# Two layers of experts behind a Fourier filter: the second layer's sums of activations wait for the next pair

## The chip, the cores and the metric

The kernel runs on one core of one Trainium2 chip. The metric is the device time of one execution in microseconds (us); the time given for a version is the median of its runs. The profile is of one further execution.

## The reference

An input of 2 x 3008 x 256 goes through a spectral filter (a Fourier transform along the sequence, a complex matrix of 256 x 256 with soft threshold, the transform back). The 6016 rows then go through two layers of dense experts, in float32. The change touches the second one alone:

```
silu = g * (1.0 / (1.0 + np.exp(-g)))      # g   = x @ w_gate, 256 -> 1536
val = x @ w_val                            # val = x @ w_val,  256 -> 1536
return (silu * val @ w_out)                # 1536 -> 256
```

## The kernel before, in words

A matrix product in float32 is made of three products of rounded parts: each operand is split in a high part (a cast on ACT) and a low part (full minus high, on DVE, `low`), and PE multiplies low x high, high x high and high x low (`mm3`). So one "product" below is three matmuls of 128 x 128 weights on up to 512 columns.

The second layer works through 6 **pairs** of token blocks (two blocks of 512 columns; 448 in the last pair), and in each pair through 12 **quads**, one per 128 of the 1536 hidden features. A quad (`quad`, one call) multiplies the 2 x 2 arrangement of (gate, value) by (two halves of 256 inputs) by (two blocks) with 7 products instead of 8, on sums that were formed beforehand. Its weights come as a slot of 18 tiles of 128 x 128 (1152 KB): 14 for the seven products, 4 for the output layer. There are four slots, fetched two quads ahead from a scratch tensor in HBM (`Wd`) that the first layer's part of the program has written.

Two quads, an even and an odd one, make a **step**: their four gated activations (two features' groups by two blocks) are again a 2 x 2 arrangement, and the output layer takes 7 products for it too. Three of them are multiplied in the step itself, or one step later (`live`, into PSUM banks `acc1`, `acc2`, `acc4`). The other four need sums of activations and sums of output weights. The activations' operands lie in `units` tiles (13 of them, two steps each, taken and given back in turn) until the *next* pair, where `part2` splits one into parts per quad and `later` multiplies it, two halves per quad, with a `chunk` of weight sums from the scratch tensor `Vd`.

The sums of output weights are formed once, during the first pair. `ask_out(k)` reads the four output tiles of a step from `Wd`: a plain DMA (issued by SP) brings the high parts, and an accumulating DMA (issued by POOL) adds the low parts on top, after the first has landed. `out_sums` forms four sums on DVE, `out_parts` splits them and writes them to `Vd`. `ask_out(k + 1)` stands behind `out_parts(k)` in the odd quad.

The sums of activations: the even quad gives T1 (`times2` at its end) and T3 (`upper`, in the next quad); the odd quad gives V, a buffer of its own, and B22. T1 is cast and multiplied, then an accumulating DMA adds T3 to it. T2 = B22 + T1 is formed on DVE (`second_t`), an accumulating DMA adds T2 to V, and V is then cast and multiplied once more as "T4". V itself was multiplied before that. A third accumulating DMA adds B22 to T3 (`upper`).

Every engine takes its instructions in the order in which this code records them (the order is written by hand); an instruction waits on semaphores, and all behind it on its engine waits too. SP and POOL issue DMAs in their own order. `last` multiplies the four late products of the last pair when no quad is left.

Lines that matter below: L937 to L939 the matmuls of a quad's products, L132 to L134 those of `live`, L1166 to L1168 those of `later`; L1291, L1305, L1331 ACT copies of a product (to Q, c7, cu); L1343 and L1361 the DVE adds that end a gate; L1344 and L1366 the silu on ACT; L1261 the cast of a live operand; L1141 the cast in `part2`; L1150 the copy of the first output product at a pair's end (`begin`); L1212 the accumulating read of output weights; L1242, L1256, L1264 the accumulating DMAs into V, T3 and T1.

Of the kernel before, what the change touches and what calls it, by code (L numbers as in the profile page):

```python
# [82 lines left out]
def fourier_moe_kernel(ctx: ExitStack, tc: tile.TileContext, x, lin, bias, w1, w2, fwd1, inv2, fwd2,  # L83
# [612 lines left out]
    class Convert2(Convert):  # L696
# [10 lines left out]
        def steps(self):  # L707
# [6 lines left out]
            for i in range(n + 1):  # L714
# [21 lines left out]
                nc.scalar.copy(t[:, 14:16], O)  # L736
                low(t[:, 7:14], F[:, 1:], t[:, :7])
                yield
                low(t[:, 16:], O, t[:, 14:16])
# [346 lines left out]
    LATER = ("T2", "T1", "B22", "T3")  # L1086
# [4 lines left out]
    def lay_out():  # L1091
        ring2["c"] = Ring(xs_p.tile([128, 3, BLK], F32, tag="ct", name="cc", bufs=1), 0, 3)
        st = [wst.tile([128, BLK], t, tag="st", name="hv", bufs=5) for t in (F32,) * 4 + (F32R,)]
        spots.update(h=st[:2], V=st[2:4], lo=st[4:])

    def lay_out_rest():
        s = [cv.tile([128, BLK], t, tag="s", name="live", bufs=3) for t in (F32R, F32R, F32R)]
# [4 lines left out]
        spots.update(hi=s[1:], v=r[:1], w=r[1:2], short=r[2:], hi2=[c[:, 0:2], c[:, 2:4]], lo2=[c[:, 4:6], e[:, :2]])  # L1102
# [14 lines left out]
    def live(p, m, k, w, e, x):  # L1117
        if k == 0:
            acc[p, m] = acc_bank([128, BLK], f"acc{m}")
        mm3(acc[p, m][:, : halves[p]], w[:, 14 + e], w[:, 16 + e], *x, k == 0, k == KF2 // 2 - 1)  # L1120
# [25 lines left out]
    def begin(p):  # L1146
        n = halves[p]
        D = C[p, "D"] = one_bank(spot[0], [128, BLK], "D")
        a = acc.pop((p, 1))
        nc.scalar.copy(D[:, :n], a[:, :n])  # L1150
        c = C[p, "short"] = take("short")
        nc.scalar.copy(c[:, :n], a[:, :n])

    def later(p, i, half, D=None):
        m, kk = divmod(i, 3)
        n = halves[p]
        hi, lo = mid[p, i]
        w = mid[p, i, "w"]
        k = 2 * kk + half
        if m == 3 and k == 0:  # L1160
            C[p, "E"] = one_bank(spot[0] if D is None else D, [128, BLK], "E")
        o = C[p, "E" if m == 3 else "D"]
        wh, wl = w[:, 2 * half], w[:, 2 * half + 1]
        o, xh, xl = pairwise(o[:, :n]), woven(hi[:, half]), woven(lo[:, half])
        start = m == 3 and k == 0
# [9 lines left out]
    def phase(p, m):  # L1175
        n = halves[p]
        D = C[p, "E" if m == 3 else "D"][:, :n]
        if m == 0:
            v = C[p, "v"][:, :n]
            nc.vector.tensor_tensor(out=v, in0=D, in1=v, op=ALU.subtract)  # L1180
        elif m == 1:
            c = C[p, "w"] = take("w")
            nc.scalar.copy(c[:, :n], D)
        elif m == 2:
            c = take("short")
            nc.scalar.copy(c[:, :n], D)
            send_out(p, 0, 1, c)
        else:
            for name, e, t in (("w", 1, 1), ("v", 1, 0)):
                c = C.pop((p, name))  # L1190
                nc.vector.tensor_tensor(out=c[:, :n], in0=D, in1=c[:, :n], op=ALU.add)
                send_out(p, e, t, c)

    def corner(p):
        n = halves[p]
        c = C.pop((p, "short"))
        nc.vector.tensor_tensor(out=c[:, :n], in0=c[:, :n], in1=acc.pop((p, 2))[:, :n], op=ALU.subtract)
        send_out(p, 0, 0, c)

    def fourth(p):  # L1200
        n = halves[p]
        c = C[p, "v"] = take("v")
        nc.scalar.copy(c[:, :n], acc.pop((p, 4))[:, :n])

    G = {}

    def ask_out(k):
        F = G[k] = cv.tile([128, 8, 128], F32, tag="full", name="outs", bufs=2)
        for i in range(2):
            t = F[:, 2 * i : 2 * i + 2].rearrange("p a b -> p (a b)")  # L1210
            nc.sync.dma_start(t, Wd[2 * k + i][:, 14 * 128 : 16 * 128])
            nc.gpsimd.dma_start(t, Wd[2 * k + i][:, 16 * 128 :], accum_op=ALU.add)  # L1212

    def out_sums(k):
        F = G[k]

        def minus(o, x, y, sign=1):
            if sign > 0:
                nc.vector.tensor_tensor(out=F[:, o], in0=F[:, x], in1=F[:, y], op=ALU.subtract)
            else:  # L1220
                nc.vector.scalar_tensor_tensor(out=F[:, o], in0=F[:, x], scalar=-1.0, in1=F[:, y], op0=ALU.mult,
                                               op1=ALU.subtract)

        minus(5, 1, 3, -1)
        minus(4, 5, 0, -1)
        minus(6, 2, 4)
# [254 lines left out]
```

## Time and profile before

| | |
|---|---|
| median of the runs shown | 1233.7 us (1233.08 the lowest) |
| profiled execution | 1236.13 us, span 1234.3 us |
| mean granted TensorE clock | 0.968 |
| busy over the span | PE 92%, DVE 78%, ACT 67%, POOL 12% |
| DMA | 264.29 MB; SP's queue 53.1%, POOL's 14.8% of 16 engines' span |
| second layer's quads | from 614.76 us to 1197.86 us, then the tail |

The span is the time from the first to the last instruction; the execution's own time lies 1.8 us above it. PE's busy time says little of its pace: matmuls are pipelined, so the distance of their starts is what counts. A share of 1.00 of the DMA engines would be all 16 at work all the time.

### The profile page before, as it was taken

What the parts mean: (1) busy time and instruction counts of PE and PEld (TensorE: products, weight loads), DVE (VectorE), ACT (ScalarE), POOL (GpSimd) and SP (SyncE); (2) the same over time, 40 slices, a digit from 0 to 9 for tenths busy, and PEclk for the clock granted to TensorE, in tenths of its full rate; (3) what the DMA queues carried; (4) which work ended last, traced back from release to release, by engine and by line L of the source; (5) the groups of instructions that cost most, each with busy time, mean ns of one, the idle gap of its engine ahead of it and who ended that gap; (6) DMA issues with size and microseconds to landing.
All of it is one profiled execution on the core that took longest, in us unless ns stands there. A gap on an engine that the chain in (4) does not pass through costs nothing.

```text
span 1234.3 us, 20183 instructions
## 1 busy us (share of the span) xinstructions
PE 1136.3 (92%) x7362; PEld 979.7 (79%) x7362; DVE 962.1 (78%) x1677; ACT 823.8 (67%) x1500; POOL 148.6 (12%) x189
## 2 busy tenths in 40 slices
PE   9999999999999999999967568999999999998896
PEld 8988888888888888889955457877777777778874
DVE  6878888999999999999845356887777776776674
ACT  4767666787878877877744246675666666665663
POOL 3000026000000000000012111111111111111120
PEclk9999999999999999999988879999999999998997
DMA  8756339654735637355467869888888888888873
GB/s 306 273 172 202 111 96 302 221 184 127 263 134 172 228 126 248 137 179 206 133 200 201 207 166 294 251 275 274 249 261 274 237 259 273 239 261 242 265 200 114
DMA packets 95307, 264.29 MB, mean 214 GB/s; under 512 B 9316, under 2 KB 35204, under 8 KB 83752
## 3 DMA queue, kind: packets, MB, share of 16 engines
q1 hardware_dynamic: 76048, 227.32, 53.1%
q0 software_dynamic: 19008, 35.59, 14.8%
q8 instruction: 58, 0.95, 0.3%
q14 instruction: 41, 0.34, 0.1%
q10 hardware_dynamic: 152, 0.08, 0.0%
HBM read 191.99 MB, written 43.25 MB: 191 GB/s over the span
## 4 chain that ended last, share of the span: by engine, by line
PE 65%; DMA 16%; DVE 8%; ACT 6%; issue 4%; POOL 0%; SPq 0%; ACTq 0%; DVEq 0%; POOLq 0%
DMA hv<-units 9%; PE acc L132 7%; PE acc L134 7%; PE acc L133 7%; PE P L937 6%; PE P L939 5%; PE P L938 5%; DMA outs<-Wd 5%; PE Tb L937 3%; PE Tb L939 3%; PE Tb L938 3%; PE p L367 1%; PE p L461 1%; PE Q L937 1%; PE p L577 1%
## 5 line engine op out<-in xcount | busy, mean ns | idle before, releaser
L1344 ACT ACTIVATE hv<-hv 128x512 f32<-128x512 f32 (+1 forms) x72 | 44.8, 622 | 146.2 <-DVE hv L1343 146.2
L617 ACT CAST gated<-r 128x512 fp32r<-128x512 f32 (+1 forms) x160 | 98.1, 613 | 64.8 <-DVE r L985 63.3
L137 DVE TENSOR_TENSOR gated<-r,gated 128x512 fp32r<-128x512 f32 (+1 forms) x160 | 107.8, 674 | 23.9 <-ACT gated L617 19.1
L132 PE MATMUL acc<-gated,w_o 128*128 128x512 f32 (+1 forms) x320 | 120.4, 376 | 0.0
L133 PE MATMUL acc<-gated,w_o 128*128 128x512 f32 (+1 forms) x320 | 119.6, 374 | 0.0
L134 PE MATMUL acc<-gated,w_o 128*128 128x512 f32 (+1 forms) x320 | 119.6, 374 | 0.0
L937 PE MATMUL P<-xo,slot 128*128 128x512 f32 (+1 forms) x240 | 92.8, 387 | 2.7 <-DVE hold L989 1.2
L981 ACT ACTIVATE r<-hold,consts 128x512 f32<-128x512 f32 (+1 forms) x120 | 85.5, 713 | 13.9 <-DVE hold L989 11.8
L938 PE MATMUL P<-xo,slot 128*128 128x512 f32 (+1 forms) x240 | 90.2, 376 | 0.0
L939 PE MATMUL P<-xo,slot 128*128 128x512 f32 (+1 forms) x240 | 90.1, 375 | 0.0
L985 DVE SCALAR_TENSOR_TENSOR r<-r,hold 128x512 f32<-128x512 f32 (+1 forms) x120 | 80.8, 673 | 2.5 <-ACT r L981 1.4
L1261 ACT CAST live<-hv 128x512 fp32r<-128x512 f32 (+1 forms) x72 | 43.8, 609 | 54.2 <-DMA hv<-units 54.2
L1141 ACT CAST parts<-units 128x1024 fp32r<-128x1024 f32 (+1 forms) x72 | 74.2, 1032 | 7.7 <-PE E L1167 3.9
L937 PE MATMUL P<-gs,slot 128*128 128x512 f32 x104 | 43.2, 416 | 35.7 <-DVE hv L1361 34.7
L132 PEld LDWEIGHTS acc<-gated,w_o 128*128 128x128 f32 x320 | 60.5, 189 | 7.0
L134 PEld LDWEIGHTS acc<-gated,w_o 128*128 128x128 f32 x320 | 60.5, 189 | 6.9
L133 PEld LDWEIGHTS acc<-gated,w_o 128*128 128x128 f32 x320 | 60.5, 189 | 6.7
L137 DVE TENSOR_TENSOR parts<-units,parts 128x1024 fp32r<-128x1024 f32 (+1 forms) x36 | 43.2, 1201 | 24.2 <-ACT parts L1141 24.2
L1361 DVE TENSOR_TENSOR hv<-P,cc 128x512 f32<-128x512 f32 (+1 forms) x72 | 48.6, 675 | 17.2 <-PE P L939 16.8
L1212 POOL DMA_DIRECT2D outs<-Wd x12 | 10.8, 1038 | 420.5 <-ACT r L981 394.8
L137 DVE TENSOR_TENSOR hv<-hv,live 128x512 fp32r<-128x512 f32 (+1 forms) x35 | 23.8, 680 | 47.5 <-ACT live L1261 47.5
L1256 POOL DMA_DIRECT2D units<-units x36 | 33.5, 931 | 224.1 <-DVE units L1246 216.4
(241 smaller groups left out, 3528.3 us busy)
## 6 DMA issues: line engine op xcount, KB each, us to landing
slot<-Wd SPq DMA_DIRECT2D x72, 1152.0 KB
slot<-Sd SPq DMA_DIRECT2D x40, 896.0 KB
chunk<-Vd SPq DMA_DIRECT2D x72, 256.0 KB
st<-in_w SPq DMA_DIRECT2D x68, 256.0 KB
units<-units POOLq DMA_DIRECT2D x60, 256.0 KB, 3.9
Wd<-slot SPq DMA_DIRECT2D x12, 1152.0 KB
hv<-units POOLq DMA_DIRECT2D x30, 256.0 KB, 7.1
m<-in_fwd SPq DMA_DIRECT2D x12, 512.0 KB
```

What stands on the lines that cost most here:

```text
L132: nc.tensor.matmul(o, wl, xh, start=start, stop=False)
L133: nc.tensor.matmul(o, wh, xh, start=False, stop=False)
L134: nc.tensor.matmul(o, wh, xl, start=False, stop=stop)
L137: nc.vector.tensor_tensor(out=o, in0=full, in1=hi.bitcast(F32), op=ALU.subtract)
L617: nc.scalar.copy(hi[:, :n], g[:, :n])
L937: nc.tensor.matmul(o, wl, hi, start=start, stop=False, skip_group_check=not start)
L938: nc.tensor.matmul(o, wh, lo, start=False, stop=False, skip_group_check=not start)
L939: nc.tensor.matmul(o, wh, hi, start=False, stop=True, skip_group_check=not start)
L981: nc.scalar.activation(r[:, :n], x[:, :n], AF.Relu, bias=three)
L985: nc.vector.scalar_tensor_tensor(out=r[:, :n], in0=r[:, :n], scalar=6.0, in1=x[:, :n], op0=ALU.min, op1=ALU.mult)
L1141: nc.scalar.copy(hi, t[:, :, :n])
L1361: nc.vector.tensor_tensor(out=h1[:, :n], in0=P[:, :n], in1=c7, op=ALU.add)
```

## The change

In the first layer's part, the four output tiles of an odd or even group are stored per output half (high, low, high, low) instead of (high, high, low, low). A fetch takes 16 of 18 tiles for even quads and in all quads of the first pair; the last two tiles of an odd group's slot are overwritten, in the first pair, with a sum of output weights that `out_sums` forms as a fifth result (`fourth`).

The three products of a step that are multiplied at once are now T1, T4 and T2, each as it comes from its own product (in the step itself, and in the next step's even quad). The four for the next pair are T1 + T3, T2 + (T1 + T3), T3 + T2 and T4 + that T2, all formed in place in `units`: two by accumulating DMAs (`add_apart`), two by DVE (`add_up`). V and its buffers are gone; the buffers serve `ask_out`, which reads two steps at the start and then stands in the even quad behind `out_sums`, for two steps (four quads) later. In the output, `phase`, `corner` and `third` combine the seven products in another order; all four late products now go into one PSUM bank, except at the very end, where `E` takes one. In even quads `later`'s second half moves ahead of product 7, and both live products stand in the even quad.

```
@@ fetch @@
-            nc.sync.dma_start(slot[q][:, :c].bitcast(F32).rearrange("p a b -> p (a b)"), src)
+            if stream[q][0] == 2 and (stream[q][1] % 2 == 0 or q < len(quads1) + KF2):
+                c = 16
+            nc.sync.dma_start(slot[q][:, :c].bitcast(F32).rearrange("p a b -> p (a b)"), src[:, : c * 128])
...
-    LATER = ("T2", "T1", "B22", "T3")
+    LATER = ("T1", "T2", "T3", "T4")
...
@@ ask_out, out_sums, out_parts @@
     def ask_out(k):
-        F = G[k] = cv.tile([128, 8, 128], F32, tag="full", name="outs", bufs=2)
+        F[k] = take("outs").rearrange("p (a b) -> p a b", b=128)
         for i in range(2):
-            t = F[:, 2 * i : 2 * i + 2].rearrange("p a b -> p (a b)")
-            nc.sync.dma_start(t, Wd[2 * k + i][:, 14 * 128 : 16 * 128])
-            nc.gpsimd.dma_start(t, Wd[2 * k + i][:, 16 * 128 :], accum_op=ALU.add)
+            t = F[k][:, 2 * i : 2 * i + 2]
+            w = Wd[2 * k + i][:, 14 * 128 :].rearrange("p (e h c) -> p e h c", e=2, h=2)
+            nc.sync.dma_start(t, w[:, :, 0])
+            nc.gpsimd.dma_start(t, w[:, :, 1], accum_op=ALU.add)
...
-        minus(5, 1, 3, -1)
-        minus(4, 5, 0, -1)
-        minus(6, 2, 4)
-        minus(7, 0, 1)
+        nc.scalar.mul(g[:, 3], A[:, 3], -1.0)
+        minus(g[:, 0], A[:, 1], A[:, 3], -1)
+        minus(g[:, 1], g[:, 0], A[:, 0], -1)
+        minus(g[:, 2], A[:, 0], A[:, 1])
+        minus(g[:, 4], A[:, 2], g[:, 1])
+        if k + 2 < KF2 // 2:
+            ask_out(k + 2)
...
+        low(f[:, 1], g[:, 4], f[:, 0])
         nc.sync.dma_start(Vd[:, :, k], t.bitcast(F32).rearrange("p m i c -> p m (i c)"))
+        nc.sync.dma_start(Wd[2 * k + 1][:, 16 * 128 :], f.bitcast(F32).rearrange("p i c -> p (i c)"))
...
-    def second_t(p, k):
-        u, v = U(p, "T2", k), state[p, "V"]
-        sub_tile(U(p, "B22", k), U(p, "T1", k), u, ALU.add)
-        nc.gpsimd.dma_start(v, u, accum_op=ALU.add)
+    def add_up(p, k, to, x):
+        o = U(p, to, k)
+        nc.vector.tensor_tensor(out=o, in0=o, in1=U(p, x, k), op=ALU.add)
+
+    def add_apart(p, k, to, x):
+        nc.gpsimd.dma_start(U(p, to, k), U(p, x, k), accum_op=ALU.add)
...
@@ upper, halve @@
-        o = U(p, ("T3", "B22")[odd], k)
-        times2(o, h[:, :n], P[:, :n], 1 if odd else -1)
-        if odd:
-            nc.gpsimd.dma_start(U(p, "T3", k), o, accum_op=ALU.add)
+        times2(U(p, ("T3", "T2")[odd], k), h[:, :n], P[:, :n], 1 if odd else -1)
...
-        if what == "T1":
-            nc.gpsimd.dma_start(x, U(p, "T3", k), accum_op=ALU.add)
@@ quad @@
+        if old >= 0:
+            later(old, i, 1)
         if odd:
-            if old >= 0:
-                later(old, i, 1)
-            x[1] = halve(p, k, "T1")
-            if pv >= 0:
-                x[4] = halve(pv, kv, "T4")
-        elif pv >= 0:
-            x[2] = halve(pv, kv, "V")
-        T = one_bank(spot[0] + 3, [128, BLK], "Tb")
-        product(T, 7, start=True)
+            x1 = halve(p, k, "T1")
+            add_apart(p, k, "T1", "T3")
+            if a[0] >= 0:
+                add_up(*a, "T2", "T1")
+                add_apart(*a, "T4", "T2")
+        elif a[0] >= 0:
+            x2, x3 = halve(*a, "T4"), halve(*a, "T2")
+            add_up(*a, "T3", "T2")
+        if old >= 0 and i % 3 == 2:
+            phase(old, i // 3)
+        if old >= 0:
+            product(T, 7, start=True)
...
-        if not odd and pv >= 0:
-            second_t(pv, kv)
...
         if odd:
-            live(p, 1, k, slot[F0 + q - 1], 0, x[1])
+            live(p, 1, k, slot[F0 + q - 1][:, 14:16], x1)
             free.append(slot.pop(F0 + q - 1))
-        elif pv >= 0:
-            live(pv, 2, kv, slot[F0 + q - 1], 0, x[2])
+            fetch(F0 + q + ASK)
+        elif a[0] >= 0:
+            live(a[0], 2, a[1], slot[F0 + q - 1][:, 14:16], x2)
...
-                live(pv, 4, kv, slot[F0 + q - 2], 1, x[4])
-                free.append(slot.pop(F0 + q - 2))
...
-        elif old >= 0:
-            later(old, i, 1)
+        if not odd and a[0] >= 0:
+            live(a[0], 3, a[1], slot[F0 + q - 1][:, 16:18] if a[0] else fourth[a[1]], x3)
+            free.append(slot.pop(F0 + q - 1))
...
@@ last @@
-        order = (0, 1, 2, 9, 3, 4, 5, 10, 6, 7, 8, 11)
+        order = (0, 1, 2, 3, 4, 5, 9, 6, 7, 8, 10, 11)
...
     lay_out()
     ask_out(0)
+    ask_out(1)
```

POOL's order at the start of the first pair. L1212 before and L1216 after are the accumulating reads of output weights (`Wd_63` and `Wd_64` are the first step's); the other rows are accumulating DMAs of activations. Before:

```order
L1212 DMA outs<-Wd_63 128x256
L1212 DMA outs<-Wd_64 128x256
L1264 DMA units<-units 128x512
L1212 DMA outs<-Wd_65 128x256
L1212 DMA outs<-Wd_66 128x256
L1256 DMA units<-units 128x512
L1242 DMA hv<-units 128x512
L1264 DMA units<-units 128x512
```

And now:

```order
L1216 DMA hv<-Wd_63 128x2x128
L1216 DMA hv<-Wd_64 128x2x128
L1216 DMA hv<-Wd_65 128x2x128
L1216 DMA hv<-Wd_66 128x2x128
L1216 DMA hv<-Wd_67 128x2x128
L1216 DMA hv<-Wd_68 128x2x128
L1254 DMA units<-units 128x512
L1216 DMA hv<-Wd_69 128x2x128
L1216 DMA hv<-Wd_70 128x2x128
L1254 DMA units<-units 128x512 x2
```

The reads of three steps now stand ahead of the first sum of activations, and of the three accumulating DMAs per step two are left.

ACT's order in a later pair, around an odd quad before (`CAST live<-units` is T1, the next `CAST live<-hv` is V after its transfer, `cc<-Tb` the copy that frees product 7's bank for product 4):

```order
L1291 COPY Q<-P 128x512
L1261 CAST live<-units 128x512
L1261 CAST live<-hv 128x512
L1305 COPY cc<-Tb 128x512
L1141 CAST parts_7181<-units 128x1024
L1331 COPY cc<-P 128x512
```

And now, around an even quad (the two casts are T4 and T2):

```order
L1299 COPY Q<-P 128x512
L1270 CAST live<-units 128x512 x2
L1318 COPY cc<-Tb 128x512
L1145 CAST parts_7190<-units 128x1024
L1338 COPY cc<-P 128x512
```

No cast of a live operand reads a tile that a DMA has added to; in odd quads one cast is left.

DVE's order from an odd quad's end through the next even quad, before (L1237 is T2 = B22 + T1):

```order
L1246 TENSOR_TENSOR units<-hv,P 128x512
L137 TENSOR_TENSOR live<-hv,live 128x512
L1237 TENSOR_TENSOR units<-units 128x512
L137 TENSOR_TENSOR lows<-units,parts_7181 128x1024
L1343 TENSOR_TENSOR hv<-Tb,cc 128x512
L1361 TENSOR_TENSOR hv<-P,cc 128x512
```

And now (L1251 is T3 = T3 + T2, in place):

```order
L1258 TENSOR_TENSOR units<-hv,P 128x512
L137 TENSOR_TENSOR live<-units,live 128x512
L137 TENSOR_TENSOR lows<-units,live 128x512
L1251 TENSOR_TENSOR units<-units 128x512
L137 TENSOR_TENSOR lows<-units,parts_7190 128x1024
L1351 TENSOR_TENSOR hv<-Tb,cc 128x512
L1364 TENSOR_TENSOR hv<-P,cc 128x512
```

One low part came over from the odd quad; the add in place writes T3, which the DMA T1 = T1 + T3 of the quad before reads. The odd quad has the other add in place.

## Rows read from the trace of the kernel before

**Rows 1.** Busy time of each engine in stretches, clock, DMA share.

```profile
core 0: us, PE busy (x) PEld busy (x) DVE busy (x) ACT busy (x) POOL busy (x), PEclk, DMA share, GB/s
614.76:741.81 127.05, 84.91 (x324) 67.09 (x323) 64.53 (x116) 53.12 (x95) 23.12 (x26) 0.83 0.71 192
741.81:831.30 89.49, 84.75 (x378) 69.99 (x378) 69.38 (x100) 60.35 (x103) 15.70 (x18) 1.00 0.88 270
...
923.50:1017.19 93.69, 86.81 (x378) 72.91 (x378) 69.40 (x101) 60.84 (x103) 15.69 (x18) 0.96 0.85 258
...
1110.17:1197.86 87.69, 79.61 (x377) 72.27 (x378) 58.85 (x90) 53.28 (x96) 15.72 (x18) 0.96 0.82 243
1197.86:1234.30 36.44, 22.40 (x80) 16.93 (x79) 16.48 (x20) 13.43 (x19) 1.74 (x2) 0.79 0.39 117
745.00:780.00 35.00, 32.23 (x145) 26.34 (x144) 26.16 (x38) 22.13 (x38) 6.98 (x8) 1.00 0.93 302
411.40:492.80 81.40, 81.40 (x541) 70.39 (x543) 77.07 (x144) 65.00 (x114) 0.00 (x0) 1.00 0.56 188
```

**Rows 2.** PE's waits, first pair: for whom, us, times, longest.

```profile
PE P L937 <- DVE hv L1361: 34.7, 6, 7.4
PE P L937 <- DMA slot<-Wd: 5.6, 4, 2.4
```

**Rows 3.** Chain of waits, one step of the first pair: start, us.

```profile
672.31 3.08 DMA outs<-Wd
676.49 9.62 DMA outs<-Wd
688.60 0.79 PE P L937
```

**Rows 4.** Landing of L1212, the accumulating read of output weights.

```profile
DMA to landing us min/median/max: 3.1/9.1/10.2
```

**Rows 5.** Landing of L1264, T1 = T1 + T3.

```profile
DMA to landing us min/median/max: 3.1/3.3/8.3
```

**Rows 6.** Landing of L1256, T3 = T3 + B22.

```profile
DMA to landing us min/median/max: 3.1/6.3/10.5
```

**Rows 7.** PE's timeline in a later pair: start, us, instruction [idle before].

```profile
937.75 0.48 PE L937 MATMUL Tb<-xo,slot 128*128 128x512 f32 x1 [2.34 <-ACT cc L1305]
...
939.77 0.63 PE L938 MATMUL P<-xo,slot 128*128 128x512 f32 x1
...
943.50 0.38 PE L937 MATMUL Tb<-xo,slot 128*128 128x512 f32 x1
...
957.10 0.38 PE L937 MATMUL Tb<-xo,slot 128*128 128x512 f32 x1
```

**Rows 8.** ACT's timeline at the same place.

```profile
936.60 0.62 ACT L1261 CAST live<-hv 128x512 fp32r<-128x512 f32 x1 [3.65 <-DMA hv<-units]
937.12 0.58 ACT L1305 COPY cc<-Tb 128x512 f32<-128x512 f32 x1
```

**Rows 9.** PE's waits from 923.50 to 1017.19, a later pair.

```profile
PE Tb L937 <- ACT cc L1305: 5.5, 3, 2.3
PE D L1166 <- ACT D L1150: 1.3, 1, 1.3
```

**Rows 10.** DMA queues in the first pair: packets, MB, share of 16 engines.

```profile
q1 hardware_dynamic: 7166, 18.78, 45.2%
q0 software_dynamic: 3744, 5.51, 25.3%
```

**Rows 11.** POOL's DMA queue from 741.81 to 1197.86, five later pairs.

```profile
q0 software_dynamic: 12960, 23.07, 28.5%
```

**Rows 12.** POOL's timeline in a later pair.

```profile
952.16 0.87 POOL L1264 DMA_DIRECT2D units<-units  x1 [5.08 <-DVE lows L137]
```

**Rows 13.** DVE's timeline in the same step.

```profile
958.66 0.68 DVE L1237 TENSOR_TENSOR units<-units 128x512 f32<-128x512 f32 x1
```

**Rows 14.** PE's timeline in the tail.

```profile
1206.07 0.74 PE L132 MATMUL acc<-live,slot 128*128 128x448 f32 x1 [3.72 <-ACT live L1261]
```

More of the change, by code (lines that the diff above doesn't have):

```diff
@@ L1176, in phase @@
         n = halves[p]
-        D = C[p, "E" if m == 3 else "D"][:, :n]
+        D, one, three = C[p, 0][:, :n], C[p, "one"][:, :n], C[p, "three"][:, :n]
         if m == 0:
-            v = C[p, "v"][:, :n]
-            nc.vector.tensor_tensor(out=v, in0=D, in1=v, op=ALU.subtract)
+            nc.vector.tensor_tensor(out=one, in0=D, in1=one, op=ALU.subtract)
         elif m == 1:
-            c = C[p, "w"] = take("w")
-            nc.scalar.copy(c[:, :n], D)
+            nc.vector.tensor_tensor(out=three, in0=D, in1=three, op=ALU.add)
+            send_out(p, 0, 1, three)
@@ L1184, in phase @@
         elif m == 2:
-            c = take("short")
-            nc.scalar.copy(c[:, :n], D)
-            send_out(p, 0, 1, c)
-        else:
[L1189 to L1192, printed above, removed]
+            c = take("short")[:, :n]
+            nc.scalar.copy(c, D)
+            send_out(p, 1, 1, c)
+            if (p, "end") in C:
+                nc.vector.tensor_tensor(out=one, in0=D, in1=one, op=ALU.subtract)
+        elif (p, "end") in C:
+            nc.vector.tensor_tensor(out=one, in0=C[p, 3][:, :n], in1=one, op=ALU.add)
+            send_out(p, 1, 0, one)
+        else:
+            c = take("short")[:, :n]
+            nc.vector.tensor_tensor(out=c, in0=D, in1=one, op=ALU.subtract)
+            send_out(p, 1, 0, c)
@@ L1194, in corner, with third @@
     def corner(p):
         n = halves[p]
-        c = C.pop((p, "short"))
-        nc.vector.tensor_tensor(out=c[:, :n], in0=c[:, :n], in1=acc.pop((p, 2))[:, :n], op=ALU.subtract)
+        c = take("short")[:, :n]
+        nc.vector.tensor_tensor(out=c, in0=C[p, "one"][:, :n], in1=acc.pop((p, 2))[:, :n], op=ALU.subtract)
         send_out(p, 0, 0, c)
-    def fourth(p):
+    def third(p):
         n = halves[p]
-        c = C[p, "v"] = take("v")
-        nc.scalar.copy(c[:, :n], acc.pop((p, 4))[:, :n])
@@ L1269, in mark @@
         nc.tensor.matmul(o, slot[F0][:, 0], B[len(pairs)][1][:, 0], start=True, stop=True)
+    NK = KF2 // 2
     def quad(q, before):
@@ L1375, in last @@
         w = slot[F0 + len(quads2) - 1]
-        order = (0, 1, 2, 9, 3, 4, 5, 10, 6, 7, 8, 11)
+        order = (0, 1, 2, 3, 4, 5, 9, 6, 7, 8, 10, 11)
+        C[p, "end"] = True
+        C[p, 3] = one_bank(spot[0] + 4, [128, BLK], "E")
         def both(at):
-            i = order[at]
             for half in range(2):
-                later(p, i, half, spot[0] + 4)
-            if i % 3 == 2:
-                phase(p, i // 3)
-        def prepare(at):
-            if at > 1:
-                ask(p, order[at])
-            part2(p, order[at])
-        upper(before)
-        x = halve(p, k, "V")
-        both(0)
-        ask(p, 2)
-        part2(p, 1)
-        second_t(p, k)
-        live(p, 2, k, w, 0, x)
-        both(1)
-        part2(p, 2)
-        corner(p)
-        ask(p, order[3])
-        x = halve(p, k, "T4")
-        live(p, 4, k, w, 1, x)
-        fourth(p)
-        for at in range(2, 12):
+                later(p, order[at], half)
             if at + 2 < 12:
                 ask(p, order[at + 2])
+        both(0)
+        upper(before)
+        part2(p, 1)
+        x2 = halve(p, k, "T4")
+        both(1)
+        x3 = halve(p, k, "T2")
+        add_up(p, k, "T3", "T2")
+        add_up(p, k, "T2", "T1")
+        add_apart(p, k, "T4", "T2")
+        part2(p, 2)
+        live(p, 2, k, w[:, 14:16], x2)
+        both(2)
+        live(p, 3, k, w[:, 16:18], x3)
+        corner(p)
+        third(p)
+        phase(p, 0)
+        part2(p, 3)
+        for at in range(3, 12):
             both(at)
```

106 lines of the change are left out of this document (48 added, 58 removed).

## The prediction, made before the changed kernel ran

> **What bounds the kernel now.** I first cut the span into stages, each ending where a pair's first output product is copied out (ACT L1150), and read busy time, clock and DMA share of each [rows 1]. In the last pair of the first part PE is busy 81.40 of 81.40 us, with DVE at 77.07: PE can run without a gap beside a nearly full DVE. The second part does not reach that. Its first pair takes 127.05 us with PE busy 84.91 and a mean granted clock of 0.83; the next five take 87.69 to 93.69 us, the tail 36.44.
>
> Next, who PE waits for. In the first pair, 34.7 us in 6 waits go to the DVE add L1361 and 5.6 us to weights that have not landed [rows 2]. L1361 is not slow: the chain of waits runs from the weight sums through two transfers, 3.08 and 9.62 us, one after the other, to PE [rows 3]; the accumulating one lands after a median of 9.1 us [rows 4]. They are asked for in the quad before the one in which DVE wants them, and DVE works in order, so all behind them stands still. In a later pair PE waits 5.5 us in 3 waits for the ACT copy L1305, and 1.3 us at the border of the pairs [rows 9]. L1305 stands behind the ACT cast of V, which waited 3.65 us for V's accumulating transfer [rows 8]. Such a gap is paid twice: after 2.34 us of it matmuls take 0.63 us, the 1.2 GHz level, and only later 0.38 us again, the 2.4 GHz level [rows 7].
>
> The floor: 63 matmuls (an even and an odd quad) run from 943.50 to 957.10 without a gap [rows 7], 0.216 us each. A later pair has 378 [rows 1]: 81.6 us, and 82.9 with the border wait, which the change leaves. The first pair has 306 and finishes 42 narrower ones of the first part (448 columns, scaled to 0.189 us): 74 us.
>
> **The change, part by part.** *Weight sums asked for four quads ahead, first pair.* The two stages of reading (plain, then accumulating) had one quad of time and get four; even at 6.5 us a quad that is 26 us against the 3.1 + 9.6 of [rows 3]. So the 34.7 us go, with the half clock behind them. Next late are the DMA engines. Their share of 0.71 over 127.05 us is 90.2 us of work [rows 1]. The accumulating queue had 32.1 us of it [rows 10]. In five later pairs it spent 28.5% of 456.05 us on 90 transfers of 256 KB [rows 11], 1.44 us each; 16 such stand in the first pair (of 5.51 MB in all), which leaves 0.91 us for each of its 10 of 128 KB. After the change there are 11 of the large ones and 8 of the small, now in runs of 512 B instead of 1 KB. That run length is not in the trace; I bound it by no change (0.91) and by double (1.82), and take 1.1 since half of the bytes (the landing side) keep their layout: 24.6 us, or 7.5 less. The plain queue moved 18.78 MB in 57.4 us [rows 10], 0.327 MB per us. Twelve fetches lose 0.131 MB each (-4.8 us), one step's plain reads fall before the pair (-0.8), six writes of the fourth sum come (+2.4), and shorter runs cost between 0 and 3.2, taken as 0.8: 2.4 less. DMA work is then 80.3 us, more than PE's 74. The Trainium skill ("DMA: Bandwidth & Descriptors", Specifications) says that 512 B is the least size that still runs at line rate; by it the two surcharges vanish and 80.3 becomes 78. The best long stretch of before had a share of 0.93 over 35 us with PE busy 32.23 [rows 1]; at that share 80.3 us take 86, and with some start-up I take **90 us: 37 less**. Bounds: 80 (share 1.00) and 105 (share 0.76).
>
> *The fourth sum* adds per step a small ACT negation, a cast, a DVE difference and a write. Each DVE operation is under the 0.68 us of 512 columns [rows 13]; DVE is busy 64.53 of 127.05 us there, so I cost them at nothing; uncovered, six times 0.7 us.
>
> *V is not waited for, later pairs.* T4 is cast as it comes from its product, T2 right behind; no transfer stands between a product and its cast. The 5.5 us of waits per pair go, with the slow matmuls behind them. On ACT the cast of T2 now waits for a DVE product behind P's third product: 0.68 + 0.62 + 0.58 us until the copy L1305 is out [rows 8, 13], some 2.1 us with the hand-overs, while PE has 15 matmuls (second half of the old pair, T, Q, P, live), 3.2 us, until it needs that copy. Spare: 1.1 us. In even quads the old pair's second half moves forward, and the third live product moves there from the odd quad: 33 and 30 matmuls, the same sum. DVE gets a second in-place add per step: 6 x 0.68 = 4.1 us on 69.40 per pair [rows 1], 73.5 of some 84, or 88%, less than the 95% beside which PE ran full. POOL and the DMA engines lose a transfer per step (6 x 1.44 us) and an eighth of 1 MB per even quad: 79.6 us of work per pair [rows 1] become 69. I take **84 us** (floor 82.9 plus 1.1 for two moments a pair where DVE is late). Four pairs, 741.81 to 1110.17, took 368.4: **32 less**, bounds 37 (at the floor) and 16 (88 us each).
>
> *The last pair* (448 columns; the old pair's 72 matmuls at 512) has a floor of 306 x 0.189 + 72 x 0.216 + 1.4 = 74.8 us; I take 78 of 87.69: **10 less** (5 to 12).
>
> *The tail* has the same wait once more: 3.72 us until 1206.07 [rows 14], and the 23 matmuls that follow at half clock, 0.19 us each too long, 4.2 us. The output also ends in one add and one send instead of two. Its only new transfer, T4 += T2, is wanted by the last product alone. **9 less** (4 to 12).
>
> *The new wait.* T3 += T2 on DVE must come after the transfer T1 += T3, which still reads T3. Today's counterpart is issued at 952.16 [rows 12]; the add will stand at or one operation behind 958.66 [rows 13], 6.5 to 7.2 us later. This transfer lands after a median of 3.3 us, at most 8.3 [rows 5]. I cost it at nothing; behind it stand DVE's whole queue, ACT's silu and PE.
>
> The sum: 37 + 32 + 10 + 9 = 88 us. The span of 1234.3 becomes 1146, the profiled execution's 1236.1 becomes 1148, and the median of the runs shown lies 2.4 lower: **1146 us**. Gains at their bounds: 108 us (1126) and 47 (1187).
>
> **Rivals.** *A, the DMA engines take over.* The first pair stays at 105, and bursts make fetches late in later pairs: 88 us each, 82 for the last, tail 31. Gains 22 + 16 + 6 + 5 = 49: 1184. For it: shares of 0.85 to 0.88 already [rows 1], and 5.6 us of late weights [rows 2]. Against it: a seventh of the work leaves. The Trainium skill (same page, "Issuing engines are not separate DMA queues") says that what SP and POOL start runs on the same 16 engines and interleaves; so asking earlier buys latency and no bandwidth. By that rule the first pair cannot fall below its 80 us of transfers.
>
> *B, another hand-over replaces V's.* The 1.1 us of spare is used up by DVE, and PE waits at L1305 as often as now; only first pair and tail gain: 37 + 9 = 46, so 1188. Against it: DVE's 88%.
>
> *C, slower.* The new wait decides. If T1 += T3 lands like the transfers that now run beside fetches, up to 10.5 us [rows 6], DVE waits 3.3 us or more in each step, PE some 2.5 us of it, and as in [rows 7] the slow matmuls add 1.9: 4.4 us a step, 26 a pair. Five pairs would take 80 us more, the first pair and tail give back 46: 1233.7 + 34, about 1268. It turns at 2.9 us per step over 30 steps, a landing near 9 us; the transfer's median of 3.3 speaks against it.
>
> *D, it does little.* The first pair is DMA-bound at its present share, 80.3/0.71 = 113 us, later pairs keep their waits elsewhere, the tail gains 4: 1216.
>
> **How the numbers follow.** Forecast 0.60, A 0.19, B 0.10, D 0.06, C 0.05. The likeliest case alone spans 1128 to 1166. Until no more than 2 in 10 is left out, the range takes in A and B: **1128 to 1188**; D, C and a little at the low end are out. A measurement here tells 2% (25 us) from no change, so faster means under 1209: forecast, A and B, 0.89; D 0.06 within; C 0.05 slower.
>
> **What the next profile would show.** In the first pair: no wait of PE for DVE behind the sums' transfers, a DMA share near 0.9, length about 90 us, clock near 1. If it is near 105 with waits for weights, A. In later pairs: the row "PE Tb from ACT cc" gone or below 1 us a pair, 83 to 85 us between border copies. If the row stays, B. DVE waiting for a transfer at the in-place add in most steps, with PE waits of over 2 us each, is C, and would make the prediction wrong; so would DMA shares under 0.8 in the first pair together with long PE gaps.

## The result, and the profile after

The changed kernel takes 1172.8 us (median of 4 runs, 1167.8 to 1177.6), the kernel before 1233.4 beside it: a ratio of 0.953 [0.946, 0.960]. That is 61 us less; the forecast was 88 less (1146 us), with 1188 as its upper end. One run of the kernel before, of 3571 us, is not in the ratio. The profiled execution took 1175.5 us, with a span of 1173.3.

The stages of the changed kernel, cut as in [rows 1] at the copy of a pair's first output product (now L1154); the columns are those of [rows 1]:

```profile
613.86:708.33 94.47, 78.21 (x324) 62.45 (x323) 67.16 (x126) 54.34 (x107) 19.66 (x19) 0.95 0.75 222
708.33:798.94 90.61, 85.17 (x378) 73.01 (x378) 73.16 (x106) 59.95 (x102) 10.41 (x12) 0.96 0.80 248
798.94:886.81 87.87, 84.41 (x378) 72.08 (x378) 73.28 (x106) 59.80 (x103) 10.47 (x12) 0.98 0.80 248
886.81:972.73 85.92, 83.06 (x378) 71.04 (x378) 73.08 (x106) 59.80 (x103) 10.41 (x12) 1.00 0.82 254
972.73:1060.41 87.68, 84.41 (x378) 72.34 (x378) 72.66 (x106) 59.17 (x103) 10.44 (x12) 0.98 0.78 248
1060.41:1142.61 82.20, 76.77 (x375) 70.74 (x375) 62.56 (x96) 52.37 (x96) 10.47 (x12) 0.98 0.77 236
1142.61:1173.30 30.69, 20.47 (x81) 16.26 (x81) 17.73 (x22) 12.89 (x18) 0.86 (x1) 0.86 0.47 137
```

The first pair gave 32.6 us, the next four 16.3 (the second alone lost 1.1), the last 5.5, the tail 5.7; 0.9 came ahead of them. PE's waits in the first pair and in the five later pairs (us, times, longest):

```profile
PE P L940 <- DMA slot<-Wd: 10.9, 5, 3.0
PE Q L940 <- ACT Q L1299: 2.6, 6, 0.5
...
PE D L1166 <- ACT D L1154: 5.5, 4, 1.4
PE D L1166 <- DMA chunk<-Vd: 5.2, 1, 5.2
PE P L940 <- DVE hv L1364: 3.5, 5, 0.7
PE D L1166 <- DVE sums L1179: 2.3, 4, 0.8
```

The first two rows are the first pair's, the others the five later pairs'. The 34.7 us for DVE [rows 2] and the waits for ACT's copy of Tb [rows 9] are gone. New are the first `chunk` of the second pair and some short waits for DVE. The latter lie at one place of each pair, behind the add L1251 (T3 += T2, in place) of its third quad. POOL ahead of it in the fifth pair (the first of the two transfers is T1 += T3), the add, and PE behind it:

```profile
983.97 1.74 POOL L1254 DMA_DIRECT2D units<-units  x2 [13.71 <-DVE hv L137]
...
993.70 0.69 DVE L1251 TENSOR_TENSOR units<-units 128x512 f32<-128x512 f32 x1 [2.92 <-DMA units<-units]
...
995.05 0.48 PE L1166 MATMUL D<-parts,chunk 128*128 128x512 f32 x1 [0.70 <-DVE sums L1179]
...
996.18 0.48 PE L1168 MATMUL D<-lows,chunk 128*128 128x512 f32 x1 [0.43 <-DVE lows L137]
...
997.38 0.79 PE L940 MATMUL P<-gs,slot 128*128 128x512 f32 x1 [0.72 <-DVE hv L1364]
...
998.38 0.63 PE L942 MATMUL P<-gs,slot 128*128 128x512 f32 x1
...
1000.89 0.38 PE L942 MATMUL Tb<-xy,slot 128*128 128x512 f32 x1
```

DVE stands 2.92 us for the transfer T1 += T3, which started 9.7 us earlier. PE has work left until 994.3; then come gaps of 0.70, 0.43 and 0.72 us, and some 3 us of matmuls of 0.63 us, the 1.2 GHz level. The same add waits 1.85, 2.48, 2.52 and 2.16 us in the other later pairs; behind the 2.48 us there is a stretch at 1.2 GHz too, behind the 2.52 us none. In the whole program DVE waits there 7 times, 17.8 us; the transfers of that line land as follows:

```profile
DMA to landing us min/median/max: 3.1/6.2/12.8
```

This row mixes two transfers. Read one by one in the five later pairs, T1 += T3 lands after 3.1/3.6/9.9 us, against 3.1/3.3/8.3 in [rows 5]; T4 += T2, which POOL starts some 0.6 us behind it, lands after 4.6/8.8/12.3. The median of T1 += T3 has hardly moved; the one in a pair's second quad is late, by 8.2 to 9.9 us in each of the five pairs.

Three questions: does this wait explain the missing gain of the later pairs; what holds the first pair at 94; and was it V's wait that gave what the later pairs did gain?

### The profile page after: what moved, and what is told of

It is laid out like the page before. It is cut to its first block, busy times and chain, and to the rows that moved or that the text cites. A ratio compares the mean times of both kernels' runs of the same rounds, so it can differ in the third digit from the quotient of the medians.

```text
span 1173.3 us, 20145 instructions
## 1 busy us (share of the span) xinstructions
PE 1120.2 (95%) x7362; PEld 975.2 (83%) x7362; DVE 985.4 (84%) x1720; ACT 820.3 (70%) x1506; POOL 121.9 (10%) x153
## 4 chain that ended last, share of the span: by engine, by line
PE 49%; issue 31%; DVE 7%; DMA 5%; POOL 4%; ACT 3%; ACTq 0%; POOLq 0%; DVEq 0%
PE acc L132 6%; PE acc L134 6%; PE acc L133 6%; POOL units L1254 4%; PE P L940 3%; PE P L942 3%; PE P L941 3%; DMA units<-units 2%; PE p L461 2%; PE p L367 2%; PE Tb L940 2%; PE Tb L941 1%; PE Tb L942 1%; PE p L417 1%; DVE r L988 1%
## 5 line engine op out<-in xcount | busy, mean ns | idle before, releaser
L1254 POOL DMA_DIRECT2D units<-units x72 | 65.2, 1063 | 420.9 <-DVE hv L137 393.5
L940 PE MATMUL P<-xo,slot 128*128 128x512 f32 (+1 forms) x240 | 91.6, 382 | 5.4 <-DMA slot<-Wd 2.1
L942 PE MATMUL P<-xo,slot 128*128 128x512 f32 (+1 forms) x240 | 89.3, 372 | 0.0
L941 PE MATMUL P<-xo,slot 128*128 128x512 f32 (+1 forms) x240 | 89.3, 372 | 0.0
L1166 PE MATMUL D<-parts,chunk 128*128 128x512 f32 (+1 forms) x138 | 55.0, 399 | 17.6 <-ACT D L1154 7.3
L1270 ACT CAST live<-units 128x512 fp32r<-128x512 f32 (+1 forms) x108 | 63.7, 608 | 11.1 <-DVE units L1258 10.7
L1251 DVE TENSOR_TENSOR units<-units 128x512 f32<-128x512 f32 (+1 forms) x72 | 48.6, 674 | 17.8 <-DMA units<-units 17.8
L1216 POOL DMA_DIRECT2D hv<-Wd x12 | 14.8, 1638 | 446.8 <-DMA hv<-Wd 419.1
L940 PEld LDWEIGHTS P<-xo,slot 128*128 128x128 f32 x240 | 45.4, 189 | 16.8 <-DVE hv L1364 4.5
```

Source lines behind the costliest of these rows:

```text
L940: nc.tensor.matmul(o, wl, hi, start=start, stop=False, skip_group_check=not start)
L941: nc.tensor.matmul(o, wh, lo, start=False, stop=False, skip_group_check=not start)
L942: nc.tensor.matmul(o, wh, hi, start=False, stop=True, skip_group_check=not start)
L1254: nc.gpsimd.dma_start(U(p, to, k), U(p, x, k), accum_op=ALU.add)
```

## Experiments on the missing gain

Each kernel differs from the changed kernel in the edit that its diff shows, in part where lines are left out (`...`). Each ran beside the kernel before again (medians of 1229 to 1232 us), to which its ratio is. Stages are cut as above, in one profiled execution each; "five pairs" are the second to the sixth, 434.3 us in the changed kernel. A sum of five pairs differs by up to 6 us between kernels with the same code in them (ask_one, below), so smaller differences show nothing.

**add_odd**: the add that waits, one quad later.

```diff
             x2, x3 = halve(*a, "T4"), halve(*a, "T2")     # even quad
-            add_up(*a, "T3", "T2")
...
             if a[0] >= 0:                                 # odd quad
+                add_up(*a, "T3", "T2")
                 add_up(*a, "T2", "T1")
```

> Theory (the add): the later pairs miss their 84 us because T3 += T2 on DVE stands once a pair for the transfer T1 += T3, 17.8 us in 7 waits, and PE pays for it twice, in short gaps and in half clock. One quad later the transfer has 6.8 us more, over its longest landing of 12.8 us. DVE's waits for that transfer fall below 2 us in all; the five later pairs, 434 us together in the changed kernel, take 412 to 420; the median falls from 1172.8 to 1151 to 1158. Rival (load): DVE at 84% and bursts of weight fetches make PE's gaps; the wait moves to the next thing that is late, the five pairs stay above 429 and the median within 1168 to 1178.

Measured: 1161.3 us, ratio 0.943 [0.941, 0.946]. DVE's waits for the transfer are gone, and the five pairs take 421.5 us, 12.8 less. The fifth pair, which took 87.68 us in the changed kernel, is now

```profile
971.57:1056.45 84.88, 82.42 (x378) 71.12 (x378) 72.95 (x106) 59.42 (x103) 10.29 (x12) 1.00 0.84 255
```

The theory holds at the second to fifth pair, 8.5 us less together. The 4.3 us of the sixth aren't the add's alone: in the changed kernel PE also waits 2.1 us for weights there, with slow matmuls behind, and ask_one, with the same code in it, takes 77.3 us for that pair instead of 82.2. The median fell 11.5 us, short of the 15 to 22 expected; in the profiled execution the first pair took 3.7 us more, with 13.7 us of PE's waits for weights. PE's 5.2 us for the first chunk stay.

**fetch_early**: the odd quad's fetch at the head of the quad.

```diff
-        if not odd:
-            fetch(F0 + q + ASK)
+        fetch(F0 + q + ASK)
...
             free.append(slot.pop(F0 + q - 1))             # odd quad, behind live
-            fetch(F0 + q + ASK)
```

> Only the odd quad's fetch moves, to the head of the quad, ahead of the writes of the weight sums that SP waits for in the first pair. Theory (late issue): the first pair's DMA engines are busy 0.75 of the time while PE waits 10.9 us for weights, so the fetches come late rather than slowly; these waits fall under 4 us and the first pair from 94.5 to 86 to 90 us; later pairs keep within 2 us; median 1164 to 1169. Rival A (the DMA engines are full): the same bytes take the same time, waits for weights stay at 8 us or more, the first pair stays at 93 to 96.

Measured: 1157.7 us, ratio 0.941 [0.938, 0.944]. SP in the first pair, of the changed kernel and then of this one, shows what moved (start, us the issue took):

```profile
642.86 0.56 SPq L1246 DMA_DIRECT2D Vd<-parts  x1
643.52 0.58 SPq L1247 DMA_DIRECT2D Wd<-s  x1
644.19 1.85 SPq L862 DMA_DIRECT2D slot<-Wd  x2
```

```profile
638.29 0.42 SPq L862 DMA_DIRECT2D slot<-Wd  x1
643.03 0.56 SPq L1246 DMA_DIRECT2D Vd<-parts  x1
643.68 0.69 SPq L1247 DMA_DIRECT2D Wd<-s  x1
644.48 0.91 SPq L862 DMA_DIRECT2D slot<-Wd  x1
```

Two fetches stood behind the writes of the weight sums and started as one burst; now each starts on its own. PE's waits for slots in the first pair are gone, and the pair takes 88.8 us at a DMA share of 0.85:

```profile
612.62:701.42 88.80, 76.75 (x324) 61.31 (x323) 67.39 (x126) 53.84 (x107) 19.66 (x19) 0.96 0.85 250
```

So the fetches had come late, not slowly. Of PE's waits in the pair 6.5 us for DVE are left, behind the add. That the five pairs fell as well, to 421.0 us, neither theory expected; the median lies 6 us below the expected range with them. DVE still waits at the add once a pair, in the changed kernel and then in this one:

```profile
DVE units L1251 <- DMA units<-units: 11.9, 5, 2.9
DVE units L1251 <- DMA units<-units: 7.5, 5, 2.3
```

The longest of these waits is 2.27 instead of 2.92 us. PE's gaps behind them come to 0.5 to 1.2 us a pair instead of 1.1 to 2.0, no slow matmuls follow, and the clock of the third to sixth pair is 1.00. So a wait at the add is cheap while it is short; what the early fetch has to do with its length is not shown.

**raw_later**: the 1 MB load of the next pair's input one quad later.

```diff
-        return ([load] if load else []) + [lambda c=c: step(*c) for c in order]
+        todo = [lambda c=c: step(*c) for c in order]
+        if load:
+            todo[-2:] = [lambda: (step(*order[-2]), step(*order[-1]))]
+            todo[:0] = [lambda: None, load]
+        return todo
```

> Only the 1 MB load of the next pair's input moves, from the end of a pair's first quad to the end of its second (and what is made of it by as much). Theory (bursts): T1 += T3 is issued in the second quad behind that load and two weight fetches, and lands late for that reason; without the load ahead of it DVE's waits at the in-place add fall from 11.9 us in 5 to under 5 us in the five later pairs, and these take 418 to 427 us instead of 434. Rival (the two fetches back to back are enough, or DVE's queue is): the waits stay at 9 us or more and the pairs at 430 or more.

Measured: 1171.0 us, ratio 0.952 [0.948, 0.956]. The five pairs took 422.5 us, as the theory said, but DVE's waits fell only to 7.4 us in 4 (longest 2.46), not under 5, and the first pair took 104.1 us with PE waiting 10.3 us for DVE. So the load is a part of the burst, not all of it. Whether the moved load lengthened the first pair is not shown: there DVE waits 17.1 us in 2 for T1 += T3 at the add, but v_late, whose first pair has the changed kernel's code, shows 15.2 us of the same wait.

**full_fetch**: all 18 tiles in every fetch.

```diff
-            if stream[q][0] == 2 and (stream[q][1] % 2 == 0 or q < len(quads1) + KF2):
-                c = 16
```

> Every fetch brings all 18 tiles again, 128 KB more in 42 of 72 fetches, 5.5 MB in all; at the first pair's 0.367 MB per us that is 15 us of DMA work, some 2 us in each later pair and 4 in the first. If transfers set the time (rival A of the prediction) the median rises by 10 to 16 us to 1183 to 1189. If only their moments count, it stays within 6 us, 1167 to 1179.

Measured: 1180.2 us, ratio 0.959 [0.955, 0.962], 7.4 us more, between both expectations, with an interval that overlaps the changed kernel's. The five pairs took 431.4 us, no more than with fewer weights; the first pair 102.3. First pairs with the changed kernel's code took 92.4 (v_wait, below) to 99.0 us (v_late), and they differ by DVE's wait for T1 += T3 at the add (full_fetch, v_late, v_wait):

```profile
DVE units L1249 <- DMA units<-units: 17.0, 2, 8.7
DVE units L1251 <- DMA units<-units: 15.2, 2, 8.4
DVE units L1251 <- DMA units<-units: 5.7, 2, 4.4
```

So only a part of the 102.3 us can be the tiles' doing. The bytes of the fetches do not set the time of the later pairs at this load; what makes that wait long in some first pairs and short in others stays open.

## Experiments on what gave the gain

**ask_one**: weight sums asked for one step ahead, as before.

```diff
-        if k + 2 < KF2 // 2:                              # out_sums
-            ask_out(k + 2)
...
                 out_parts(k)
+                if k < NK - 1:
+                    ask_out(k + 1)
...
     ask_out(0)
-    ask_out(1)
```

> The weight sums are asked for one step ahead again, in the odd quad behind the parts of the step before; all else as changed. Theory (asking early is the first pair's gain): PE's waits for DVE behind these transfers return, 25 to 40 us in the first pair, which goes from 94.5 us to 118 to 130; later pairs unchanged within 3 us; median 1197 to 1208. Rival (the fewer weights and the in-place sums gave it): the first pair stays under 105 us and the median under 1184.

Measured: 1205.4 us, ratio 0.979 [0.977, 0.981], 32.7 us more. The first pair, and PE's longest wait in it:

```profile
618.83:746.61 127.78, 83.17 (x324) 66.65 (x323) 67.33 (x126) 55.51 (x107) 22.12 (x21) 0.84 0.58 168
```

```profile
PE P L940 <- ACT cc L1338: 39.4, 5, 8.0
```

Its 127.8 us are the 127.05 of before [rows 1], half clock included. Asking early is the whole gain of the first pair. The five pairs, whose code is the changed kernel's, were to stay within 3 us and took 428.3, 6.0 less, of which 4.9 lie in the last: so far does equal code differ from one profiled execution to another. PE's wait has ACT's name now, since it is ACT that meets the accumulating read first (L1228 negates one of its tiles):

```profile
ACT outs L1228 <- DMA hv<-Wd: 45.0, 5, 9.1
```

**v_wait** and **v_late** bring back, from the second pair on, the hand-over in which a product waits for a transfer: T4 is cast again in the odd quad, behind T4 += T2. The third live product, and behind it the odd quad's fetch, stand in the odd quad with it. T4 with its sum is multiplied where the result wants T2, so these kernels compute something else. In v_wait the sums stand early in the even quad; v_late puts them behind the quad's second product, where they stood before the change.

```diff
-            x2, x3 = halve(*a, "T4"), halve(*a, "T2")     # even quad
-            add_up(*a, "T3", "T2")
+            x2 = halve(*a, "T4")
+            add_up(*a, "T3", "T2")                        # v_late: these three
+            add_up(*a, "T2", "T1")                        # behind product(Q, 2)
+            add_apart(*a, "T4", "T2")
...
-                add_up(*a, "T2", "T1")                    # odd quad
-                add_apart(*a, "T4", "T2")
+                x3 = halve(*a, "T4")                      # live(.., 3, ..) here too
```

> In pairs two to six T2 += T1 and T4 += T2 go into the even quad, and the product of T4 is multiplied in the odd quad behind that transfer, as before the change (so T4 plus sums is multiplied where the result wants T2, in this part the output differs). If the removed wait was worth what the prediction took (some 7 us a pair with its slow clock), the five later pairs rise from 434 us to 455 to 470 and the median to 1193 to 1208, with PE waiting for ACT's copy again, 4 us or more a pair. If the gain in these pairs came from fewer transfers and fewer weights instead, they stay at 430 to 445 and the median under 1183.

Measured: 1171.4 us, ratio 0.951 [0.949, 0.953]; five pairs 429.3 us. ACT waits 14.1 us for the transfer, PE 2.4 us for ACT's copy.

> As v_wait, but the three sums of T3, T2 and T4 now stand behind the quad's second product on DVE, where T2 and V were summed before the change, so the transfer into T4 starts as late as the one into V did. (T4 plus sums is again multiplied where the result wants T2.) If the wait for V was worth some 7 us a pair because it came late, ACT's waits for the transfer rise from 14 us in v_wait to 35 or more in the five later pairs, PE waits 12 us or more for ACT's copy, and the five pairs take 442 to 465 us (434 in the changed kernel, 429 in v_wait). If the transfer now lands in time because one in three is gone and fewer weights are fetched, ACT waits under 22 us, the five pairs take 420 to 433.

Measured: 1169.6 us, ratio 0.950 [0.946, 0.954]; five pairs 425.7 us. With a transfer between product and cast again, PE waits 1.2 us for ACT's copy. ACT's wait for the transfer, in the five pairs of the kernel before and of v_late:

```profile
ACT live L1261 <- DMA hv<-units: 51.6, 21, 4.0
ACT live L1270 <- DMA units<-units: 10.9, 13, 1.7
```

So the hand-over alone costs nothing that shows: the transfer lands in time. (v_late lies below the changed kernel; its add of T3 stands later, and waits 2.4 us in 2 instead of 11.9 in 5.)

**v_three** goes on from v_late: T3 += T2 is a transfer once more, just ahead of the one into T4.

```diff
+        if odd and p and (p, "end") not in C:             # upper
+            add_apart(p, k, "T3", "T2")
...
-            add_up(*a, "T3", "T2")                        # behind product(Q, 2)
-            add_up(*a, "T2", "T1")
+            add_up(*a, "T4", "T1")
             add_apart(*a, "T4", "T2")
```

> As v_late, with the third accumulating transfer of a step back as well: T3 += T2 is a transfer again, started where the one of B22 into T3 was, some 1.5 us ahead of the one into T4 on the same queue, and DVE forms T4 += T1 in its place (T2 stays without T1, and T4 plus sums is multiplied where the result wants T2, so the output differs). Theory (the wait for V was the third transfer's work: V's stood behind it on POOL's queue and landed after 6.2 us, against 3.6 in v_late): ACT waits 30 us or more for the transfer in the five later pairs, PE 10 us or more for ACT's copy, the pairs take 440 to 460 us against 426 in v_late. Rival (what eased the wait is something else in the new order, such as both halves of the old pair ahead of product 7): ACT's wait stays under 20 us and the pairs under 431.

Measured: 1195.9 us, ratio 0.975 [0.971, 0.978]; five pairs 454.7 us, 29 more than v_late and within 1.4 of the 456.05 of the kernel before. (The second pair, with the wait for its chunk, takes 5.7 us more than before, the other four 7.1 less.) In these pairs, ACT's wait and PE's longest waits, and PE's longest before:

```profile
ACT live L1272 <- DMA units<-units: 42.5, 21, 3.6
PE Tb L940 <- ACT cc L1324: 22.9, 14, 2.5
PE D L1166 <- ACT D L1154: 5.3, 4, 1.4
PE D L1166 <- DMA chunk<-Vd: 5.2, 1, 5.2
...
PE Tb L937 <- ACT cc L1305: 24.3, 14, 3.1
```

One case, on POOL, ACT and PE:

```profile
912.51 0.84 POOL L1254 DMA_DIRECT2D units<-units  x1 [5.86 <-DVE units L1258]
914.75 0.85 POOL L1254 DMA_DIRECT2D units<-units  x1 [1.39 <-DVE units L1251]
922.30 0.62 ACT L1272 CAST live<-units 128x512 fp32r<-128x512 f32 x1 [3.38 <-DMA units<-units]
923.46 0.80 PE L940 MATMUL Tb<-xo,slot 128*128 128x512 f32 x1 [2.46 <-ACT cc L1324]
```

The transfer into T4 starts 2.2 us behind the one into T3, and ACT has it 7.6 us after its issue. The wait of [rows 8] is back as soon as the third transfer of a step is. In v_late the transfers start one at a time and land after a median of 3.5 us; in v_three the two that start about 1.5 us apart land after 5.3 (the first) and 5.9 (the second), before the change after 6.1 and 5.6. The first is late as well, so standing behind another transfer isn't all of it. A kernel that keeps three transfers but takes V's hand-over away was not run.

## A better version

**three** joins add_odd, fetch_early and an earlier start for the second pair's first chunks.

```diff
+        if p == 0 and f == NF - 1:                        # behind the copy of Q
+            out_parts(k)
+            ask(0, 0)
+            ask(0, 1)
         if before:
             upper(before)
...
-            else:                                         # at product(P, 6)
+            elif k < NK - 1:
                 out_parts(k)
-                if k == NK - 1:
-                    ask(0, 0)
-                    ask(0, 1)
```

> Three edits together: T3 += T2 one quad later, the odd quad's fetch at the head of the quad, and the last step's weight sums split and the next pair's first chunks asked for at the head of the last odd quad. Theory: they cure different waits. With the early fetch alone the first pair still had 6.5 us of PE's waits for DVE behind the add (88.8 us), the second pair 4.5 us for its first chunk with half clock behind it (89.6 us). The first pair should take 81 to 85 us, the second 83 to 86, the five later pairs 413 to 417 together, the median 1142 to 1149. Rival (the early fetch already gave what the add could give, since both moved the later pairs by 13 us): only the chunk's 4 to 7 us come off, median 1150 to 1155; if the DMA engines bound the first pair it stays at 87 us or more.

Measured: 1147.9 us, ratio 0.934 [0.930, 0.937]. First pair 85.2 us at a DMA share of 0.90, second 85.4, five pairs 413.0. DVE's waits at the add of the later pairs, PE's for weights in the first pair and PE's for the first chunk are gone, so each edit cured its own wait; the first pair, with 3.1 us of DVE's waits for T1 += T3 left, came out 0.2 us above what was expected.

**best** adds two edits.

```diff
+        if f == NF - 1:                                   # ahead of product(T, 4)
+            begin(p)
         product(T, 4)
...
-        if f == NF - 1:                                   # at the quad's end
-            begin(p)
...
-            if at + 2 < 12:                               # last, both
-                ask(p, order[at + 2])
+            if at + 3 < 12:
+                ask(p, order[at + 3])
...
+        ask(p, order[2])
         both(0)
```

> The kernel three with two more edits: the copy of a pair's first output product stands right behind that product's last matmul instead of at the quad's end, and in the tail chunks are asked for three products ahead instead of two. three has 9.2 us of PE's waits for that copy at five borders, 2.2 us more at the tail's start, and 2.2 us for chunks in the tail. If these waits are on the path, the five later pairs fall from 413 to 403 to 408 us, the tail from 31.1 to 27 to 30, the median from 1147.9 to 1134 to 1142. If the DMA engines (0.86 to 0.88 of the time) or DVE take over, each wait only moves, and the median stays above 1144.

Measured: 1136.5 us, ratio 0.925 [0.923, 0.928], with 406.8 us for the five pairs, as expected: by the two ratios some 34 us below the changed kernel, and 93 below the one before. Its third and fifth pair, and its tail:

```profile
781.99:864.02 82.03, 82.03 (x381) 71.18 (x380) 73.34 (x106) 59.71 (x102) 10.70 (x13) 1.00 0.89 266
945.90:1027.78 81.88, 81.88 (x380) 71.12 (x379) 72.69 (x106) 59.47 (x101) 10.27 (x13) 1.00 0.89 265
1103.10:1132.40 29.30, 19.01 (x86) 14.59 (x84) 20.20 (x25) 13.88 (x19) 1.32 (x2) 0.98 0.58 162
```

A pair's 378 matmuls at the 0.216 us of [rows 7] are 81.6 us: PE is busy for the whole of these two pairs, and what is left lies in the first two pairs and the tail. The DMA engines at 0.89 did not hold it up.

## Why the prediction came out as it did

The time lay in the range and on the forecast side, but the forecast of 1146 was 27 us too low, and the cause given for one of its terms was incomplete. One of its own signs of being wrong came up in part: a share under 0.8 in the first pair beside gaps of PE (0.75, gaps up to 3.0 us). The 83 to 85 us between border copies were missed (86 to 91).

**First pair, 37 predicted, 32.6 measured.** The mechanism is shown by ask_one. "Next late are the DMA engines" failed. I had summed 80.3 us of DMA work; the share of 0.75 over 94.47 us is 70.9. The accumulating queue came out as summed (25.4%, 24.0 us for 24.6); the plain queue needed 49.7%, 47.0 us for 17.24 MB, where I had scaled the 0.327 MB per us of [rows 10] and it ran at 0.367. The pair ended late for another reason, SP's order: the odd quad's fetch stood behind writes that wait for DVE. I had moved the sums' reads past queues, but had not asked what the fetch itself was behind. The Trainium skill ("DMA: Bandwidth & Descriptors", "Issuing engines are not separate DMA queues") says that what different engines start runs on the same 16 DMA engines and interleaves; I took from it that asking earlier buys no bandwidth. No run here contradicts that, but it was not what bound the pair: fetch_early moves 22.1 MB in 88.8 us at a share of 0.85, where the changed kernel moves 20.9 MB in 94.5, because engine time had been left unused; three takes 85.2 us at 0.90. Near 0.9, as forecast, is where a first pair of 85 us lies, not one of 94. (PE's floor of 74 us was too high: [rows 1] has 324 matmuls in the stage, of which the trace shows 22 narrow ones and not 42, some 69 us. Nothing hung on it.)

**Four later pairs, 32 predicted, 16.3 measured**, its lower bound. Two things are missing from the sum. The new wait, which I "cost at nothing": T1 += T3 was to have 6.5 to 7.2 us and had landed in 3.3 by its median before, but what counts is the worst of six in a pair, and one in each pair landed too late. Even the 8.3 us that [rows 5] gives as the latest would have said so. add_odd shows 8.5 us over the second to fifth pair. This is rival C's mechanism once a pair instead of in each step, at 2.1 us an event (8.5 over four) instead of the 4.4 that I had put on it. (C's own sum is off by 10 us: 30 steps at 4.4 are 132 us against 88 of gains, which gives 1278 and not 1268.) The first chunk of the second pair is the other: 5.2 us, with half clock behind it. Its weight sums are formed and written in the last odd quad, and I did not follow that queue into the next pair; three takes the second pair to 85.4, where add_odd, without the wait at the add but with that for the chunk, takes 89.5. With both waits gone three's four pairs take 336.3 us, the 4 x 84 of the forecast.

**The reason for the later pairs' gain was incomplete.** I put nearly all of their 8 us a pair down to "V is not waited for". The wait was worth most of that: v_three has it back and takes 29 us more than v_late over five pairs, 5.8 a pair. But it did not need the new hand-over to go: v_late hands over as before and loses nothing, since it has two transfers a step instead of three. The change did both at once, took V's hand-over away and turned one of the three transfers into a DVE add; the second alone is shown to be enough, the first alone was not run. So the runs do not show that the prediction's reason was wrong, only that it was not needed. The prediction had the saved transfer in its text ("POOL and the DMA engines lose a transfer per step"), as load, 79.6 to 69 us a pair (measured 0.78 to 0.82 of 86 to 91 us, 68 to 73), and not as the thing that made V's transfer late. What v_three does not separate is the queue's order from the engines' load; both go with the third transfer.

**The rest.** DVE's 73.5 us a pair came out at 72.7 to 73.3 and the fourth sum cost nothing that shows (ask_one contains it and takes 127.8 us). Last pair and tail gave 5.5 and 5.7 of 10 and 9: in the tail the clock is still 0.86, and PE waits for DVE, ACT and a chunk in turn. Rival A's 88 us a pair was met by number, but not by its cause: full_fetch carries more bytes through the later pairs at no cost that shows.

## What to carry to other kernels

Where a transfer on a queue is waited for, look first at what was put on the queue just ahead of it: in the later pairs here, taking that away did as much as the whole change, in which the one who waits was moved as well. Cost a new wait by its latest landing, not its median, at the place in the program where other transfers start. In this first pair a DMA share of 0.75 beside waits for weights meant that the transfers started late: read the issuing queue's order before counting bytes.

## What the runs showed of the hardware

An accumulating transfer of 256 KB lands after 3.0 to 14.3 us (v_late's L1254). Its median differs with what POOL starts around it: 3.5 us one at a time (v_late), 5.3 and 5.9 for two about 1.5 us apart (v_three), 3.6 and 8.8 for two 0.6 us apart (the changed kernel). The busy time that a queue's packets take is no fixed price per byte: 0.327 MB per us on the plain queue in the first pair before, 0.367 after, 0.357 in fetch_early. Waits of DVE of 1.0 to 2.3 us once a pair (fetch_early) cost PE gaps of 0.5 to 1.2 us and no slow matmuls; in the changed kernel 2.48 and 2.92 us were each followed by some 3 us at the 1.2 GHz level, 2.52 us by none.
